# Longer load rows and a finer last weight piece in a decode kernel that streams 162 MB

## The chip, the cores and the metric

The kernel runs on one core of one Trainium2 chip. The metric is the device time of one execution in microseconds, lower is better.

## The reference, cut to what matters

One token goes through attention with a key/value cache and through a gated mixer, and a sigmoid gate blends the two.

```python
x = A_x                                   # 1 x 1 x 1024, bf16
q = x @ wq                                # wq 1024 x 4096: 32 heads of 128
p = softmax(q k^T / sqrt(128))            # k_cache 4 groups x 65536 x 128
a = (p @ v) @ wo                          # v_cache the same shape; wo 4096 x 1024
b = mixer(x; w_in 1024 x 3584, w_out 1792 x 1024)
out = g * a + (1 - g) * b
```

Keys and values are 67 MB each. With 28 MB of weights the core reads 162.0 MB once, and each byte is used for few operations. The loads set the time.

## The kernel before

The cache is cut into 16 tiles of keys and 16 of values, each 4 MB (128 partitions x 32 KB). On-chip memory holds three slots for key tiles and one double slot, `VB`, which in turn holds the query weights, the mixer weights, pairs of value tiles and output weights. All loads stand in one list, `stream`, and go to one hardware queue in this order. Offsets count 2-byte elements.

```python
SUB = 16384                       # one slot: 16384 elements, 32 KB a partition
GRAN = 2048                       # bookkeeping grain of the slots, in elements

load([("wq", 0)], rows(A_wq, 0, 8), VB)               # 64 KB a partition
...                                                   # keys 0, 1, mixer input (56 KB), keys 2, 3, mixer output
for i in range(6):
    load_k(2 * i + 4)
    load_v2(2 * i)                                    # a pair of value tiles, 64 KB a partition
    load_k(2 * i + 5)
load_v2(12)                                           # the seventh pair
load([("v", 14)], ...); load([("v", 15)], ...)        # into key slots
for i in range(3):
    load([("wo", i, 0)], rows(A_wo, i, 8), VB + 8 * DO * i)
s3 = kring()                                          # a key slot
for c0, c1 in [(0, 4), (4, 6), (6, 8)]:               # the last output weights, in eighths
    load([("wo", 3, c0)], rows(A_wo, 3, 8)[:, DO * c0:DO * c1], s3 + DO * c0)   # DO = 1024
```

A load is recorded as soon as every grain that it will overwrite has been used. It stops there if one has not, and `done` goes on when something more has been used:

```python
def grains(off, w):
    return list(range(off // GRAN, (off + w + GRAN - 1) // GRAN))

def issue():
    while issued[0] < len(stream):
        keys, off, src = stream[issued[0]]
        w = src.shape[1]
        gr = grains(off, w)
        if any(k not in used for x in gr if x in owner for k in owner[x]):
            return
        for x in gr:
            owner[x] = keys
        for c in range(0, w, SUB):                    # wider rows are cut: one load per 32 KB
            m = min(SUB, w - c)
            P("SP", lambda e, ...: e.dma_start(arena[:, o:o + m], src),
              w=[("slot", x) for x in grains(off + c, m)], dma="s%d" % grains(off + c, m)[0])
        issued[0] += 1

def done(key):
    used.add(key)
    issue()
```

`P` records an operation with the keys that it reads and writes and makes the semaphore waits from them. The attention loop takes a pair of value tiles per turn, and the output weights come last:

```python
for i in range(6):
    a = 2 * i + 4
    k_step(a, ...)                     # transpose (VectorE) and multiply (TensorE) a key tile
    pv_piece(2 * i)                    # TensorE: value tile, then done(("v", n))
    pv_piece(2 * i + 1)
    k_step(a + 1, ...)
...
for i, c0, c1 in [(0, 0, 8), (1, 0, 8), (2, 0, 8), (3, 0, 4), (3, 4, 6), (3, 6, 8)]:
    sl, keys = use(("wo", i, c0))
    ...                                # TensorE: 4 matmuls per eighth
    done(("wo", i, c0))
P("DVE", ...)                          # the sum to bf16, then the store
```

## Time and profile before

| | before |
|---|---|
| time, median of 5 (lowest to highest) | 383.73 us (383.66 to 383.97) |
| queue 1: packets, share of 16 engines | 6200, 98.8% |
| last weights landed | 379.50 us |
| busy TensorE, VectorE | 61%, 55% |

From the page of the kernel before: the DMA engines' busy tenths in 40 slices of the span and what they moved, the load queue and the instruction queue (packets, MB, share of 16 engines), and the group of the value matmuls (busy time, mean ns | idle time before them and what ended most of it).

```profile
DMA  9999999999999999999999999999999999999995
GB/s 384 439 435 425 423 417 435 439 436 433 439 425 418 432 430 439 439 432 432 429 420 429 435 439 434 429 435 426 422 432 437 435 432 429 439 425 420 423 425 220
...
q1 hardware_dynamic: 6200, 162.01, 98.8%
q8 instruction: 8, 0.13, 0.1%
...
L246 PE MATMUL obt<-arena 128*64 128x512 bf16 (+2 forms) x334 | 64.6, 428 | 30.6 <-DMA arena<-in_A_v_cache_dram 12.4
```

The queue is full to the last slice. TensorE waits 12.4 us for values, but that costs nothing while the queue stays full. In the packet records, 16 engines hold 16 packets on average from 1.0 us to the end of the stream.

The end of the chain of waits (start us, duration us, what):

```profile
351.47 28.03 DMA arena<-in_A_wo_dram
379.50 0.04 issue
379.54 0.63 PE fbt L706 x8
380.17 0.02 issue
380.19 0.42 DVE arena L712
```

The last piece was issued at 351.47 us and landed at 379.50. Eight matmuls and a cast follow. The queue's own waits (us in total, times, longest; the four largest sums):

```profile
SPq L365 <- PE obt L248: 234.1, 14, 29.8
SPq L365 <- DVE arena L476: 80.7, 6, 16.8
SPq L714 <- DVE arena L712: 28.7, 1, 28.7
SPq L365 <- PE mbt L535: 20.3, 3, 7.7
```

The sixth pair, tiles 10 and 11: its halves landed at 301.56 and 311.27 us. The timeline of TensorE shows the first matmuls of tile 10 and of tile 11, and the queue's timeline the issue of the seventh pair's first half with the three loads after it:

```profile
305.60 0.41 PE L246 MATMUL obt<-arena 128*64 128x512 bf16 x2
...
311.40 0.41 PE L246 MATMUL obt<-arena 128*64 128x512 bf16 x2 [2.16 <-DMA arena<-in_A_v_cache_dram]
```

```profile
309.28 8.77 SPq L365 DMA_DIRECT2D arena<-in_A_v_cache_dram  x4
```

Tile 10 took 3.48 us, from 305.60 to 309.08, where the next tile's first matmul could follow. The load that it frees room for was issued at 309.28, and its turn came at 318.69. (That is the first packet after as many bytes as all earlier loads have, counted in order of start. The engines are not in step: the first of them closed the load before it at 318.39.) It had some 9 us to spare. The stretches around it (start:end us, length, busy time and count of PE, PEld, DVE, ACT, POOL, then the granted TensorE clock, DMA share, GB/s):

```profile
306.00:311.00 5.00, 3.24 (x31) 0.69 (x12) 1.01 (x3) 0.00 (x0) 0.00 (x0) 1.00 0.98 419
311.00:314.00 3.00, 2.60 (x16) 0.86 (x10) 0.00 (x0) 0.00 (x0) 0.00 (x0) 0.65 1.06 459
314.00:317.00 3.00, 3.00 (x22) 0.96 (x10) 0.00 (x0) 0.00 (x0) 0.00 (x0) 0.78 0.96 415
```

### The profile page before, as it was taken

Reading aid. Unit: us, or ns where it says so; the run is one execution under the profiler, and the core shown is the slowest. Engines: PE = TensorE matmul, PEld = TensorE weight load, DVE = VectorE, ACT = ScalarE, POOL = GpSimd, SP = SyncE. Lnnn points to the kernel's source line nnn. Section 1 sums busy time; section 2 is a strip of 40 time slices with the busy share of each in tenths; the row PEclk is TensorE's granted clock in tenths of the full one; section 3 lists DMA queues with packets and bytes.
Section 4 is the critical chain, followed back from the end, with each engine's and each line's share of the span. In section 5 each row is a group of like instructions: output and inputs, shape, how many; then the busy total and the mean of one; then the engine's idle time right before and its main releaser. Section 6 shows DMA issues by size and latency. Waiting matters only on the chain.

```text
span 382.3 us, 2522 instructions
## 1 busy us (share of the span) xinstructions
PE 234.6 (61%) x1375; PEld 56.9 (15%) x785; DVE 211.7 (55%) x229; ACT 25.3 (7%) x39; POOL 1.5 (0%) x8
## 2 busy tenths in 40 slices
PE   0055754286687578545793777377938673849344
PEld 0011111111121111101120112012201121112121
DVE  6116952785781698067935980579448914842020
ACT  1000000102030001000210010001200100031000
POOL 1000000000000000000000000000000000000000
PEclk9996998689979599959898998786979988778695
DMA  9999999999999999999999999999999999999995
GB/s 384 439 435 425 423 417 435 439 436 433 439 425 418 432 430 439 439 432 432 429 420 429 435 439 434 429 435 426 422 432 437 435 432 429 439 425 420 423 425 220
DMA packets 6246, 162.16 MB, mean 424 GB/s; under 512 B 728, under 2 KB 732, under 8 KB 988
## 3 DMA queue, kind: packets, MB, share of 16 engines
q1 hardware_dynamic: 6200, 162.01, 98.8%
q8 instruction: 8, 0.13, 0.1%
q14 instruction: 2, 0.02, 0.0%
q10 hardware_dynamic: 36, 0.00, 0.0%
HBM read 162.01 MB, written 0.00 MB: 424 GB/s over the span
## 4 chain that ended last, share of the span: by engine, by line
DMA 61%; PE 19%; DVE 18%; SPq 1%; ACT 1%; issue 1%
DMA arena<-in_A_k_cache_dram 33%; DVE arena L476 13%; DMA arena<-in_B_w_in_dram 8%; DMA arena<-in_A_wo_dram 7%; DMA arena<-in_B_w_out_dram 6%; PE obt L246 6%; DMA arena<-in_A_wq_dram 6%; PE obt L248 5%; PE scp L246 4%; PE scp L248 4%; DVE arena L493 1%; SPq L365 1%; DVE arena L514 1%; DVE arena L464 1%; DVE arena L549 0%
## 5 line engine op out<-in xcount | busy, mean ns | idle before, releaser
L476 DVE STREAM_TRANSPOSE arena<-arena 128x2048 f32<-128x2048 f32 x64 | 145.5, 2295 | 84.5 <-DMA arena<-in_A_k_cache_dram 71.9
L246 PE MATMUL scp<-arena 128*128 128x512 bf16 x256 | 112.5, 439 | 83.4 <-DVE arena L476 61.0
L248 PE MATMUL scp<-arena 128*128 128x512 bf16 x256 | 111.0, 434 | 0.0
L246 PE MATMUL obt<-arena 128*64 128x512 bf16 (+2 forms) x334 | 64.6, 428 | 30.6 <-DMA arena<-in_A_v_cache_dram 12.4
L248 PE MATMUL obt<-arena 128*64 128x512 bf16 (+2 forms) x334 | 64.1, 424 | 0.0
L246 PEld LDWEIGHTS scp<-arena 128*128 128x128 bf16 x256 | 27.5, 107 | 192.2 <-DVE arena L476 93.8
L509 ACT ACTIVATE arena<-arena 128x1024 bf16<-128x1024 f32 x16 | 18.4, 1148 | 237.5 <-DVE arena L505 127.4
L246 PEld LDWEIGHTS obt<-arena 128*64 128x64 bf16 (+1 forms) x334 | 19.4, 116 | 86.6 <-issue 79.1
L493 DVE TENSOR_SCALAR_CACHE_REDUCE arena<-scp 128x1024 f32<-128x1024 f32 x16 | 19.3, 1205 | 9.3 <-PE scp L248 9.3
L514 DVE STREAM_TRANSPOSE arena<-arena 128x1024 bf16<-128x1024 bf16 x16 | 19.4, 1214 | 9.0 <-PE obt L248 6.4
L706 PE MATMUL fbt<-arena 128*1 128x256 bf16 x128 | 6.2, 339 | 5.9 <-DMA arena<-in_A_wo_dram 5.7
L539 DVE RECIPROCAL arena<-mbt 128x1 f32<-128x1 f32 x4 | 0.6, 139 | 14.0 <-PE mbt L535 14.0
L441 DVE CAST arena<-obt 97x1024 bf16<-97x1024 f32 x1 | 1.2, 1224 | 11.5 <-PE obt L248 11.5
L712 DVE CAST arena<-fbt 97x256 bf16<-97x256 f32 x1 | 0.4, 425 | 11.3 <-PE fbt L706 11.3
L588 DVE COPY arena<-obt 128x896 f32<-128x896 f32 x1 | 1.1, 1093 | 9.1 <-PE obt L248 9.1
L464 DVE COPY arena<-arena 32x32 bf16<-32x32 bf16 x16 | 2.7, 166 | 6.2 <-PE scp L248 6.0
L407 PE MATMUL scp<-arena 8*128 8x1 bf16 x8 | 0.6, 197 | 8.4 <-DVE arena L402 8.4
L706 PEld LDWEIGHTS fbt<-arena 128*1 128x1 bf16 x128 | 2.8, 93 | 8.8 <-DMA arena<-in_A_wo_dram 6.7
L595 ACT ACTIVATE arena<-arena 128x28 f32<-128x28 f32 x1 | 0.2, 226 | 52.4 <-DVE arena L594 52.4
L549 DVE SCALAR_TENSOR_TENSOR arena<-obt,arena 128x512 bf16<-128x512 f32 x4 | 3.0, 751 | 0.1
L601 PE MATMUL mbt<-arena 128*128 128x1 f32 x2 | 0.4, 260 | 4.3 <-DVE arena L600 4.3
L509 ACT ACTIVATION_READ_ACCUMULATOR arena<-arena 128x1 f32 x16 | 3.0, 186 | 0.0
(88 smaller groups left out, 47.0 us busy)
## 6 DMA issues: line engine op xcount, KB each, us to landing
arena<-in_A_k_cache_dram SPq DMA_DIRECT2D x16, 4096.0 KB, 38.4
arena<-in_A_v_cache_dram SPq DMA_DIRECT2D x16, 4096.0 KB, 31.1
arena<-in_A_wq_dram SPq DMA_DIRECT2D x2, 4096.0 KB, 16.8
arena<-in_A_wo_dram SPq DMA_DIRECT2D x3, 2048.0 KB, 22.6
arena<-in_B_w_in_dram SPq DMA_DIRECT2D x1, 4096.0 KB, 25.2
arena<-in_B_w_out_dram SPq DMA_DIRECT2D x1, 3584.0 KB, 23.1
arena<-in_B_w_in_dram SPq DMA_DIRECT2D x1, 3072.0 KB, 32.2
arena<-in_A_wo_dram SPq DMA_DIRECT2D x1, 1024.0 KB, 26.5
```

The costliest lines, as they stand in the source:

```text
L246: return e.matmul(*a, **kw)
L248: one = e.matmul(*a, **kw).ins
L365: P("SP", lambda e, o=OFF["RING"] + off + c, m=m, src=src[:, c:c + m]: e.dma_start(arena[:, o:o + m], src), w=[("slot", x) for x in grains ...
L441: P("DVE", lambda e: e.tensor_copy(psb[0:97, :], ob[0:97, :]), w=["psb", "ob"])
L464: P("DVE", lambda e, pb=pb: e.tensor_copy(vw(qpad, 24 + 32 * pb, [[QP, 4], [1, 8]], 32 * pb, 32), vw(qall, 8 * g, [[32, 4], [1, 8]], 32 * ...
L476: P("DVE", lambda e: e.transpose(ktb(i).bitcast(F32), sl[:, 4096 * p:4096 * (p + 1)].bitcast(F32)), r=keys[2 * p:2 * p + 2], w=[("kt", i % ...
L493: P("DVE", lambda e: e.tensor_scalar(scs(n), sc_ps(n), 0.0, None, op0=ALU.add, op1=ALU.max, accum_out=maxc[:, n:n + 1]), w=[("sc", n % NSC ...
L509: P("ACT", lambda e: e.activation(psb, scs(n), ACTF.Exp, bias=gcol(n // NP, K_NB), scale=SCALE, accum_out=lp[:, n:n + 1]), r=[("sc", n % N ...
L514: P("DVE", lambda e: e.transpose(ptsb(n), psb), r=["psb"], w=[("ptsb", n % 2)])
L549: P("DVE", lambda e: e.scalar_tensor_tensor(osc, ob[:, 512:1024], gcol(g, K_FB), osc, op0=ALU.mult, op1=ALU.add), r=[("fh", g, 1), "psb"], ...
L588: P("DVE", lambda e: e.tensor_copy(vw(zr, 0, [[FB4, 2], [32, FC], [1, 32]]), vw(ob, 0, [[512, 2], [1, FC], [FC, 32]])), w=[KZR, "ob"])
L706: ins = e.matmul(fb[32 * q:32 * q + 1, 0:QW], ovec[:, 8 * i + c:8 * i + c + 1], sl[:, o:o + QW], start=False, stop=(i == 3 and c == 7), ti ...
```

## The change

The intent is to make fewer packets, since each row of a load is one packet with some fixed cost, and to leave less TensorE work behind the last landing. Query weights, mixer input and six value pairs load as whole rows of 56 to 64 KB. The last output-weight piece of two eighths becomes two pieces of one.

```diff
-    for c0, c1 in [(0, 4), (4, 6), (6, 8)]:
+    for c0, c1 in [(0, 4), (4, 6), (6, 7), (7, 8)]:
         load([("wo", 3, c0)], rows(A_wo, 3, 8)[:, DO * c0:DO * c1], s3 + DO * c0)

+    whole = {("wq", 0), ("win", 0)} | {("v", 2 * i) for i in range(6)}
@@ issue()
-            for c in range(0, w, SUB):
-                m = min(SUB, w - c)
+            step = len(keys) * w if keys[0] in whole else SUB
+            for c in range(0, w, step):
+                m = min(step, w - c)
@@ the output weights
-    for i, c0, c1 in [(0, 0, 8), (1, 0, 8), (2, 0, 8), (3, 0, 4), (3, 4, 6), (3, 6, 8)]:
+    for i, c0, c1 in [(0, 0, 8), (1, 0, 8), (2, 0, 8), (3, 0, 4), (3, 4, 6), (3, 6, 7), (3, 7, 8)]:
```

## The prediction

> **What bounds the kernel.** The one load queue. The page shows queue 1 at 98.8% of the 16 DMA engines' span, 162.0 MB, 424 GB/s; DMA leads the chain of waits at 61%. In the packet records the engines hold nearly 16.0 packets at any time from 1.0 to 379.05 us: the queue never runs dry. The load issues agree: each waits 5 to 32 us in the queue behind earlier ones. Compute matters only where it delays an issue by more than that, and after the last landing at 379.5 us.
>
> **Costs.** Median packet times by row size: 4 KB 159 ns, 8 KB 312, 16 KB 614, 24 KB 915, 28 KB 1067, 32 KB 1216: a line of 0.0367 ns per byte plus about 11 ns. Sixteen engines at that slope move 435 GB/s, the fabric ceiling in the Trainium skill (DMA: Bandwidth & Descriptors, "Where 436 GB/s comes from"); the fixed part is of the kind in its "Why small descriptors are slow". The trace agrees with both. Packets overlap by some 3 ns; 4 MB follows 4 MB every 9.72 us, so the effective fixed cost is 9 to 10 ns a row.
>
> **Removed.** Query weights, mixer input and six pairs go from two packets per row to one: 1024 of 6200 packets, 64 per engine, x 9 to 10 ns = 0.6 us, all on the critical resource. This assumes that a 64 KB row travels as one packet of about 2418 ns (extrapolated). If it is cut into 32 KB, nothing is gained here.
>
> **Added.** The last output-weight rows are two of 2 KB instead of one of 4 KB: 8 more packets per engine, 0.1 us. Behind the last landing TensorE runs 4 matmuls instead of 8; before, the second four started 0.17 us after the first, so 0.17 us are saved.
>
> **Moved.** The first tile of a pair could be multiplied when its half had landed; now both wait for the pair (at most 9.7 us more), and the next pair is issued once, after both. A tile takes 3.45 us at full clock, up to 6.9 at half, so both need 7 to 14 us after the landing, with 19.4 us of other loads queued behind it: still 5 us or more ahead of need. The tightest place is the seventh pair (still in halves): before, its first half was issued at 309.3 us and started at 318.7. Now it follows the sixth pair's landing (311.3) by 3.5 to 5.5 us: 315 to 317, with about 1 us from issue to first packet (as at the start): 0.5 to 2.5 us to spare. Query and mixer weights need both halves anyway.
>
> **Sum.** 383.8 - 0.6 + 0.1 - 0.2 = about 383.1 us, range 382.4 to 383.9. Faster by over 2%: 1%; within 2%: 97%; slower: 2%.
>
> **What would show it.** Queue 1 with about 5200 packets; packets of 56 and 64 KB of about 2118 and 2418 ns; last landing near 378.9 us; 0.4 us of matmuls after it; DMA at nine tenths throughout; TensorE's waits for value loads grown from 12 us to some 30, at no cost; the seventh pair's first half issued near 315 us, without a gap in the packets near 318.
>
> **What would make it wrong.** Long packets running at another rate, or cut up (383.6 to 383.9); a gap where the seventh pair comes too late (1 to 3 us slower); a spread of completion between engines (2 us at the end before) that grows with long rows.

## More of the kernel before

The clock was 1.00 while tile 10 ran. It fell to 0.50 at 311.89, after 2.16 us in which TensorE was idle, and tile 11 ran at half clock until 315.31.

Where time and span are both listed, the time is 1.27 to 1.40 us longer than the span that the profile shows, so times are compared with times and traces with traces.

## The result, and the profile after

The changed kernel took 385.93 us, median of 5 (385.55 to 386.40), against 383.73 before. The ratio is 1.0057, 95% interval 1.0045 to 1.0069: slower by 2.2 us, where 0.6 us less had been forecast. A ratio is the mean time of one kernel's fast runs over that of the other's of the same rounds, so not quite the ratio of the medians.

The lines of the page of the changed kernel that answer to those shown before:

```profile
DMA  9989999999989999999999999999999999999993
GB/s 436 436 382 436 438 433 423 422 409 482 436 389 433 481 431 395 436 474 440 395 417 470 436 402 407 429 453 437 416 431 457 436 409 395 429 435 436 429 412 119
...
q1 hardware_dynamic: 5192, 162.01, 98.1%
q8 instruction: 8, 0.13, 0.1%
...
L246 PE MATMUL obt<-arena 128*64 128x512 bf16 (+2 forms) x334 | 67.5, 455 | 38.1 <-DMA arena<-in_A_v_cache_dram 29.2
```

There are 1008 packets fewer, as intended. The rates swing more from slice to slice; I take this for the coarser unit of a 64 KB packet, which no run tests. What stands out is the last slice: 119 GB/s instead of 220. The end of the chain of waits shows why:

```profile
349.16 29.04 DMA arena<-in_A_wo_dram
378.20 0.04 issue
378.24 0.60 PE fbt L708 x8
378.84 0.04 issue
378.88 0.41 PE fbt L708 x4
379.29 0.02 issue
379.31 2.67 DMA arena<-in_A_wo_dram
381.98 0.04 issue
382.02 0.41 PE fbt L708 x4
382.44 0.02 issue
382.46 0.42 DVE arena L714
```

The last load starts at 379.31 us, after the four matmuls of the eighth before it. It takes 2.67 us for 256 KB on a queue that is empty. The four largest sums of the queue's own waits name the wait, which the kernel before did not have:

```profile
SPq L367 <- PE obt L248: 211.6, 9, 37.0
SPq L367 <- DVE arena L478: 65.6, 6, 13.2
SPq L367 <- PE mbt L537: 59.2, 3, 28.2
SPq L367 <- PE fbt L708: 29.2, 1, 29.2
```

The reason stands in the code. An eighth is 1024 elements, a grain 2048. The seventh eighth begins at `s3 + 6144` and the last at `s3 + 7168`, which is the same grain. The owner of that grain is then the seventh eighth, and `issue()` returns until that has been used. The load is therefore recorded after the matmuls that read the grain, and on the chip it waits for them. The two pieces touch no common byte; only the bookkeeping joins them. Every earlier piece was a whole number of grains.

The sixth pair changed as well. These are the same views as before: TensorE's timeline, the queue's timeline, and the stretches.

```profile
310.74 0.64 PE L246 MATMUL obt<-arena 128*64 128x512 bf16 x2 [5.47 <-DMA arena<-in_A_v_cache_dram]
```

```profile
316.95 4.75 SPq L367 DMA_DIRECT2D arena<-in_A_v_cache_dram  x4
```

```profile
306.00:311.00 5.00, 0.26 (x2) 0.13 (x2) 0.61 (x3) 0.00 (x0) 0.00 (x0) 0.81 0.76 328
311.00:314.00 3.00, 3.00 (x16) 0.73 (x8) 0.00 (x0) 0.00 (x0) 0.00 (x0) 0.50 0.99 426
314.00:317.00 3.00, 3.00 (x22) 0.62 (x10) 0.00 (x0) 0.00 (x0) 0.00 (x0) 0.68 1.01 437
```

TensorE stood idle for 5.47 us until the whole pair had landed. Its clock was then 0.50, and tile 10 took 6.01 us instead of 3.48. The seventh pair's first load was issued at 316.95, and by the same count of bytes its turn came at 318.34. The first engine had closed key tile 15 at 317.90, only 0.95 us after the issue. Some engines then stood idle (0.11 us per engine on average between 316.5 and 320.5 us), and several packets that started between 317.96 and 318.57 us took 1.5 to 1.9 us instead of 1.22.

Landings of the same load in both traces show how the gain came and went (us from the span's start; a load has landed with the last of its 16 completions, read here as one from each of the 16 engines):

| load | before | after | difference |
|---|---|---|---|
| key tile 15, the last before the seventh pair | 320.98 | 320.40 | -0.58 |
| value tile 13, the second half of the seventh pair | 340.40 | 339.83 | -0.57 |
| value tile 14 | 350.12 | 349.88 | -0.24 |
| value tile 15 | 359.84 | 359.59 | -0.25 |
| output weights, eighths 5 and 6 of the last part | 378.26 | 378.20 | -0.06 |
| last output weights | 379.50 | 381.98 | +2.48 |

So 0.58 us were saved, more than half of it was lost after 340 us, and 2.5 us came at the very end. Near 318 us no landing was late. There it was the first of the 16 completions that fell back: at key tile 15 it came 0.51 us earlier than in the kernel before, at the next load 0.10 us.

### The profile page after: what moved, and what is told of

It reads as the page before. It is cut to its first block, busy times and chain, and to the rows that moved or that the text cites. A ratio compares the mean times of both kernels' runs of the same rounds, so it can differ in the third digit from the quotient of the medians.

```text
span 384.6 us, 2507 instructions
## 1 busy us (share of the span) xinstructions
PE 230.3 (60%) x1375; PEld 55.4 (14%) x785; DVE 211.2 (55%) x229; ACT 25.3 (7%) x39; POOL 1.5 (0%) x8
## 3 DMA queue, kind: packets, MB, share of 16 engines
q1 hardware_dynamic: 5192, 162.01, 98.1%
## 4 chain that ended last, share of the span: by engine, by line
DMA 76%; PE 18%; DVE 4%; issue 0%; ACT 0%; ACTq 0%; SPq 0%
DMA arena<-in_A_v_cache_dram 39%; DMA arena<-in_A_k_cache_dram 11%; PE obt L246 8%; DMA arena<-in_A_wo_dram 8%; PE obt L248 8%; DMA arena<-in_B_w_in_dram 8%; DMA arena<-in_B_w_out_dram 6%; DMA arena<-in_B_b_sp_dram 5%; DVE arena L478 2%; PE fbt L708 0%; DVE arena L516 0%; ACT arena L511 0%; DVE arena L495 0%; ACTq L271 0%; SPq L367 0%
## 5 line engine op out<-in xcount | busy, mean ns | idle before, releaser
L246 PE MATMUL scp<-arena 128*128 128x512 bf16 x256 | 105.8, 413 | 72.2 <-DVE arena L478 60.2
L248 PE MATMUL scp<-arena 128*128 128x512 bf16 x256 | 104.7, 409 | 0.0
L246 PE MATMUL obt<-arena 128*64 128x512 bf16 (+2 forms) x334 | 67.5, 455 | 38.1 <-DMA arena<-in_A_v_cache_dram 29.2
L248 PE MATMUL obt<-arena 128*64 128x512 bf16 (+2 forms) x334 | 66.9, 452 | 0.0
L246 PEld LDWEIGHTS scp<-arena 128*128 128x128 bf16 x256 | 26.2, 102 | 173.3 <-DVE arena L478 94.0
```

What stands on the lines that cost most here:

```text
L246: return e.matmul(*a, **kw)
L248: one = e.matmul(*a, **kw).ins
```

## The experiments

Theory A: the shared grain delays the last load, and that is the loss. Rival B: the long rows, or the later release of pairs, cost the time. Four kernels ran, 5 rounds each, with the kernel before at 383.70 us (383.56 to 384.24).

**Long rows without the finer tail (e1_rows_only).** The whole change, but with the old pieces:

```diff
-    for c0, c1 in [(0, 4), (4, 6), (6, 7), (7, 8)]:
+    for c0, c1 in [(0, 4), (4, 6), (6, 8)]:           # and the same in the loop that uses them
```

> The change with the last output-weight pieces put back to 4, 2, 2 eighths. Theory A (the last eighth shares a 2048-element bookkeeping grain with the seventh, so its load is issued only after the seventh is multiplied): the loss goes, and the long rows show their own worth, 0.6 us of saved fixed cost less about 0.3 us for the short gap before the seventh pair: 383.3 to 383.6 us, last landing near 379.2 us. Theory B (long rows, or the later release of the pairs, cost the time): it stays near 385.9 us.

Measured: 383.67 us (383.02 to 384.95, six executions), ratio 1.0000 (0.9987 to 1.0013). The loss is gone, so B falls. The gain that A expected did not show in the median, which missed the forecast by a little, and the spread of 1.9 us asked for a reason of its own.

**The finer tail without long rows (e2_tail_only).** The kernel before, with the pieces 4, 2, 1, 1.

> The kernel before with nothing but the last output-weight pieces in 4, 2, 1, 1 eighths. Theory A: the last load is issued after the seventh eighth's matmuls, some 2.6 us after the other six, and lands 2.7 us after that: 385.9 to 386.5 us, the queue waiting about 29 us for the matmuls of the output weights. Theory B: 383.6 to 383.8 us, no such wait.

Measured: 385.99 us (385.97 to 386.14), ratio 1.0059 (1.0047 to 1.0071). The queue's own waits of this run have the line again:

```profile
SPq L365 <- PE fbt L706: 28.7, 1, 28.7
```

The tail alone makes the whole loss.

**The whole change, last eighth in its own grain (e3_tail_apart).**

```diff
-        load([("wo", 3, c0)], rows(A_wo, 3, 8)[:, DO * c0:DO * c1], s3 + DO * c0)
+        load([("wo", 3, c0)], rows(A_wo, 3, 8)[:, DO * c0:DO * c1], s3 + DO * (8 if c0 == 7 else c0))
```

> The whole change, with the last eighth put 2048 elements further on, into a bookkeeping grain of its own (the space is free), nothing else. Theory A: all output-weight loads are issued together near 350 us, the last lands near 379.2 us, and the time is 383.1 to 383.5 us. Theory B: 385.9 us as before this edit.

Measured: 383.73 us (383.27 to 384.10), ratio 0.9998 (0.9986 to 1.0010). The line for the output matmuls is gone from the queue's waits, and the last weights landed at 379.43 us. Moving one piece by 2048 elements takes the loss away. The time is a little above the forecast range of 383.1 to 383.5, as it was in e1.

**The finer tail alone, last eighth in its own grain (e4_tail_only_apart).** The edit of e3, on the kernel of e2.

> The kernel before with the pieces 4, 2, 1, 1 and the last eighth in a grain of its own. What the finer tail is worth without the accident: 0.17 us less TensorE after the last landing, 0.08 us more for 8 rows per engine: 383.5 to 383.75 us, no change that 5 rounds can show. If smaller rows at the end cost more than their 9 to 10 ns (for instance a fixed cost per load), it is over 383.9 us.

Measured: 383.59 us (383.53 to 383.93), ratio 0.9997 (0.9985 to 1.0009). Against e2 the shared grain cost 2.40 us (385.99 - 383.59). Whether the finer tail is worth its forecast tenth of a microsecond, 5 rounds don't tell.

That settled the loss. Open was why the long rows gained nothing. Theory C: they save about 0.6 us, but the sixth pair's later release makes the seventh pair's load too late. Rival D: long rows are worth nothing. Again with the kernel before at 383.69 us (383.50 to 383.89).

**Five long pairs instead of six (e5_five_pairs).** As e3, with `range(5)` in `whole`, so that the sixth pair loads as halves.

> As the run with the last eighth apart, but the sixth pair (tiles 10 and 11) loads as two halves again, so only five pairs are long rows. Theory C (six whole pairs save 0.6 us, but the seventh pair's first load is then issued only about 1 us before it is needed, at a granted clock of 0.5 during tile 10, and the queue runs dry for 0.3 to 1 us, differently in each execution): no gap near 318 us, that load issued near 310 to 313 us, spread below 0.5 us, 383.0 to 383.3 us, 0.3 to 0.7 us under the other run of this call. Theory D (long rows are worth nothing on the clock): 383.6 to 383.8 us, as with six pairs.

Measured: 383.08 us (383.02 to 383.36), ratio 0.9985 (0.9972 to 0.9999). The load is issued early again, even ahead of the 310 to 313 us expected:

```profile
308.93 8.75 SPq L367 DMA_DIRECT2D arena<-in_A_v_cache_dram  x4
```

The median is 0.27 us under that with six pairs (next run), a little less than the 0.3 to 0.7 us that C forecast, and the two intervals overlap. The gain over the kernel before, 0.61 us, is about what the saved rows and the finer tail are worth; D is outside its range.

**Six long pairs once more (e6_tail_apart_2).** The kernel of e3.

> The run with the last eighth apart and six long pairs once more, for a comparison in the same rounds and a second trace. 383.3 to 384.1 us with the same spread of about 0.8 us; the seventh pair's first load issued at 316.5 to 318 us, and a gap near 318 us, under both theories.

Measured: 383.35 us (383.18 to 383.65), ratio 0.9992 (0.9979 to 1.0004). The spread was smaller than expected. In the profiled execution the load was issued at 316.19 us, ahead of the 316.5 to 318 expected, and waited 2.04 us for its turn: no gap there. I had expected one in this trace, so the gap is a matter of tenths of a microsecond in each execution.

**The sixth pair alone as long rows (e7_pair6_only).** The kernel before with `whole = {("v", 10)}`.

> The kernel before with the sixth pair alone as long rows. Theory C: 8 rows per engine saved, 0.08 us, against the gap: 383.8 to 384.5 us with a wider spread than before's. Theory D: 383.7 us, no gap.

Measured: 384.32 us (383.59 to 385.16), ratio 1.0015 (1.0002 to 1.0027). Eight rows per engine fewer, and slower with a spread of 1.6 us, as C forecast. But the interval only just excludes no loss, and the same kernel later (e11) does not confirm it. The trace also says that not all of this is the gap: the landing of key tile 15 was already 0.38 us behind that of the kernel before (321.36 against 320.98 us), ahead of the late load, and the last landing 0.68 us (380.18 against 379.50).

**All loads as rows of 16 KB (e8_rows_16k).**

```diff
-            for c in range(0, w, SUB):
-                m = min(SUB, w - c)
+            for c in range(0, w, SUB // 2):
+                m = min(SUB // 2, w - c)
```

> The kernel before with every load cut at 16 KB rows, each piece a load of its own: 296 more packets per engine, nothing waits for later data than before. At 9 to 10 ns a row: 2.7 to 3.0 us more, 386.4 to 386.8 us; queue 1 never dry. If the fixed cost of a row is hidden where the queue is deep: 383.7 to 384.3 us.

Measured: 386.60 us (386.57 to 386.65), ratio 1.0076 (1.0064 to 1.0089). 2.91 us for 296 rows more on each engine: 9.8 ns a row. Since each piece is a load of its own, 37 completion packets more per engine (median 9 ns) are in that figure; over all 333 packets it is 8.7 ns each. The fixed cost is real on a full queue.

What made tile 10 slow? The Trainium skill says (TensorE: Matmul & The Clock Gate, "What's actually happening") that the clock falls to half after at least one idle window of about 3.4 us, and that the window runs free (the traces bear out the length, not that the window must be idle; see the last section). That would make the wait for the whole pair, 5.5 us, the cause of the half clock (Theory E). Rival F: the load is late because of the later landing itself. The test keeps TensorE busy during the wait. The kernel before had 383.75 us (383.47 to 384.25).

**The sixth pair alone, TensorE kept busy (e9_warm_pair6).** Ahead of `pv_piece(10)`:

```diff
+    def keep_warm(m):                                  # m = 24, result unused
+        j = (nkt[0] - 1) % NKT
+        def f(e):
+            for x in range(m):
+                ins = mm(e, x > 0, sc_ps(15)[:, 0:512], qpad[:, 0:128], ktb(j)[:, 0:512],
+                         start=True, stop=True, skip_group_check=True)
+            return ins
+        P("PE", f, r=["qpad", ("kt", j)], w=[KSC(15)])
```

> The kernel with the sixth pair alone as long rows, plus 24 matmuls whose result nobody uses (they write the score bank of tile 15 before its first real matmul clears it) put before tile 10's multiplication, so that TensorE is busy for about 5.2 us of the 5.5 us in which it waits for the whole pair. Theory E (the wait for the whole pair lets the granted clock fall to 0.5, tile 10 then takes about 6 us instead of 3.45, and this alone makes the next load too late): the clock stays at 1.0 from 306 to 315 us, tile 10 takes 3.5 us, the seventh pair's first load is issued near 315 us, no gap near 318 us, 383.5 to 383.7 us with a spread under 0.4 us, against about 384.3 us without. Theory F (the later issue comes of the wait for the landing itself, whatever the clock): issue at 316 us or later, gap and 383.8 to 385 us as before.

Measured: 383.72 us (383.70 to 383.80), ratio 1.0000 (0.9987 to 1.0014). This is just above E's range, and with the added work the spread was 0.10 us. The stretches and the queue's timeline of this run:

```profile
306.00:311.00 5.00, 4.66 (x22) 0.00 (x0) 0.81 (x3) 0.00 (x0) 0.00 (x0) 1.00 0.93 400
311.00:314.00 3.00, 2.60 (x24) 0.80 (x14) 0.00 (x0) 0.00 (x0) 0.00 (x0) 1.00 1.06 459
314.00:317.00 3.00, 3.00 (x30) 0.81 (x14) 0.00 (x0) 0.00 (x0) 0.00 (x0) 1.00 0.91 393
```

```profile
315.09 4.73 SPq L367 DMA_DIRECT2D arena<-in_A_v_cache_dram  x4
```

The clock stayed at 1.00, tile 10 took 3.48 us, and the load was issued at 315.09 us, in time.

**Six long pairs, TensorE kept busy (e10_warm_six).** The same 24 matmuls in the kernel of e3.

> Six long pairs, the last eighth apart, and the same 24 unused matmuls. Theory E: as with five pairs, 383.0 to 383.1 us, spread under 0.4 us, no gap near 318 us. Theory F: 383.3 to 383.8 us with a gap in some executions.

Measured: 383.30 us (383.15 to 383.48), ratio 0.9990 (0.9977 to 1.0002). No gap, spread 0.33 us, load issued at 314.84 us. The median is 0.2 us above E's forecast, at the lower edge of F's, and above what five pairs gave. Nor is it clearly under six pairs without the added matmuls (383.35 in e6, 383.73 in e3). I have no reason for that; the times do not show what the clock is worth with six pairs.

**The sixth pair alone again (e11_pair6_again).** The kernel of e7, for the comparison in the same rounds.

> The sixth pair alone as long rows, without the added matmuls, in the same rounds as the comparison: 383.6 to 385.2 us, median about 384.3, under both theories.

Measured: 384.04 us (383.49 to 384.42), ratio 1.0005 (0.9993 to 1.0018), so 0.3 us above e9, with a spread of 0.93 against 0.10 us. The intervals of the two overlap, so it is the traces that must decide. The same stretches in its profile:

```profile
306.00:311.00 5.00, 0.00 (x0) 0.00 (x0) 0.72 (x3) 0.00 (x0) 0.00 (x0) 0.70 0.87 374
311.00:314.00 3.00, 2.85 (x14) 0.67 (x8) 0.00 (x0) 0.00 (x0) 0.00 (x0) 0.50 1.14 492
314.00:317.00 3.00, 3.00 (x26) 0.74 (x12) 0.00 (x0) 0.00 (x0) 0.00 (x0) 0.87 0.89 382
```

The same wait without the added matmuls, and the clock is at 0.50. The traces side by side, worked out from the packet and instruction records: tile 10's matmuls, the issue of the seventh pair's first load, its wait for its turn (by the count of bytes), and the engine time lost there (idle engine time between 316.5 and 320.5 us plus the excess of packets over the usual time between 316 and 321 us, per engine).

```
                    tile 10 starts, takes   issue    waits   loss   time of that execution
before                 305.60   3.48        309.28    9.42   0.00   -
five pairs             305.24   3.48        308.93    9.19   0.00   383.08
kept warm, pair 6      311.40   3.48        315.09    3.52   0.01   383.71
kept warm, six         311.16   3.48        314.84    3.36   0.00   383.30
six, again             311.00   4.98        316.19    2.04   0.04   383.18
pair 6, again          311.15   5.25        316.61    2.05   0.10   383.49
six, tail apart        311.21   5.75        317.16    1.14   0.47   383.35
the change             310.74   6.01        316.95    1.38   0.43   385.93
pair 6 alone           311.70   5.77        317.67    1.19   0.52   384.32
rows only              310.98   6.45        317.63    1.02   0.67   383.87
```

A load issued with some 2 us left costs at most 0.1 us of engine time. With 1.4 us or less it costs 0.43 to 0.67 us, in idle engines (0.11 to 0.39 us) and in packets that run longer (0.28 to 0.32 us; why they do is not shown). Where tile 10 takes 3.48 us, there is no loss, whether it starts at 305 or at 311 us. So what makes the load too late is the clock (E), not the landing alone (F). How long tile 10 takes varies from 4.98 to 6.45 us with where the windows of half clock lie, which fits a window that runs free.

Engine time lost is not yet kernel time. The engines are some 2 us apart, and a landing is the last of 16 completions. Near 318 us it is the engines ahead that lose: in the changed kernel the first and the last completion of a load lay 2.03 us apart at key tile 15 and 1.63 us at the next load. From key tile 15 to eighths 5 and 6 of the last output weights, landings fell back against the kernel before by 0.52 us in the changed kernel, 0.78 in rows only, 0.25 in pair 6 alone and only 0.04 in six with the tail apart, and by 0.02 us at most in the traces with 2 us or more left. They fell back in the stretches in which the instruction queue moved a packet, near 344 and 372 us. That these packets then meet engines which have no lead left is read from the order in time, not tested. So a late load takes away a lead, and that became time in three of four traces.

## Why the prediction was wrong, point by point

**What bounds the kernel: right.** Time followed the packets, as e8 shows.

**The saved rows: right.** The prediction said 64 rows x 9 to 10 ns = 0.6 us, with 64 KB rows of about 2418 ns. Queue 1 shows 5192 packets (forecast about 5200). Those of 64 KB took 2420 ns (median), those of 56 KB 2116. The first completion of key tile 15 came 0.51 to 0.62 us earlier in all five traces with six long pairs. That its landing was 0.58 us earlier in the changed kernel is partly luck: in the other four it was 0.09 to 0.33 us, because the last engine decides. e8 measured 9.8 ns a row, and five pairs gained 0.61 us (383.69 - 383.08; 56 rows, and the finer tail).

**The step that failed.** "The last output-weight rows are two of 2 KB instead of one of 4 KB: 8 more packets per engine, 0.1 us." This counted the new load as one more in a full queue, and "last landing near 378.9 us" rests on it. In its place there was a new wait: the last load was issued only after the matmuls of the piece before it, at 379.31 us instead of some 351, and landed 2.67 us later on an empty queue. e2 and e4 put the price at 2.40 us. It could have been read from the code without a profile: 1024-element pieces against `GRAN = 2048`. The prediction costed the packets of the new piece and never asked whether its issue condition was still met. The Trainium skill (DMA: Bandwidth & Descriptors, "Anatomy of one DMA — SWDGE (gpsimd) path") gives about 2.0 us plus bytes / 436 GB/s for one load issued from GpSimd, which this one is not; for 256 KB that is an estimate of 2.6 us, close to the 2.67 measured here. Taken out of the full queue, the load cost the kernel 2.40 us of it.

**A term that was mis-sized.** "Now it follows the sixth pair's landing (311.3) by 3.5 to 5.5 us: 315 to 317 [...] 0.5 to 2.5 us to spare." The place was right, the size was not: in the six traces with the wait and no added matmuls tile 10 took 4.98 to 6.45 us, the issue followed the pair's landing by 5.2 to 6.7 us and came at 316.19 to 317.67 us, and 0.43 to 0.67 us of engine time were lost in four of them. The prediction knew that half clock doubles the time of a tile, but not that the wait it had just introduced was what halves the clock. The traces of e9 and e10 show that it was. The 17 us that TensorE waited more for values (29.2 against 12.4, forecast "some 30, at no cost") cost nothing that e5 would show in five pairs; in the sixth they used up the time to spare.

**The smaller tail: open.** Behind the last landing, the chain before shows 0.69 us to the cast (380.19 - 379.50), after it 0.48 (382.46 - 381.98): 0.21 us less in the traces, where 0.17 were forecast, but 5 rounds of e4 don't resolve it against its 8 rows more.

**What stays open.** The forecast of busy loads "at nine tenths throughout" failed in the last slice, for the reason given; the eight tenths in two earlier slices, with no gap in the packet records, I take for the coarser packets. In the traces with a loss of 0.47 us or more near 318 us, the last 4 KB packets were slower by 0.2 to 0.4 us per engine on average (e1, e3, e7). I have not found why. The changed kernel's other 0.2 us, between value tile 15 and the last pieces but one, fall where the 16 completions of a load move from 1.98 to 2.17 us apart, after an instruction packet at 371.85 us; that is not tested either. A risk that the prediction named did not show: at key tile 15 the completions lay 2.03 to 2.63 us apart with six long pairs, and 2.11 to 2.57 us in the three traces with rows of 32 KB at most.

**The better version.** Five long pairs with the last eighth in its own grain (e5) ran at 383.08 us, 0.15% under the kernel before, and its interval just excludes no gain.

## What to carry to other kernels

When a load is cut finer, check what decides when it may be issued (grain, slot, semaphore) before counting its packets: one load that left a full queue cost 2.40 us here, nearly its whole round trip of 2.67. Merging loads delays what waits for their first part; look for the one place where the next load is nearly due, and size it with the clock that the longer wait will leave. Look at the last of the 16 completions as well as at the mean: a gap on engines that are ahead need not cost time. Row length itself is a small lever once rows reach 32 KB: some 10 ns out of 1216.

## What the Trainium skill lacked or had wrong

- DMA: Bandwidth & Descriptors, "Where 436 GB/s comes from": its ceiling of 435 GB/s agrees. The slope over the median packets of 2 to 64 KB, 0.0368 ns per byte on each of 16 engines, is 435 GB/s. "Why small descriptors are slow" gives some 3 cycles of fixed overhead per packet; if these are cycles of the 850 MHz fabric, which the page does not say, that is about 3.5 ns (an estimate). Measured on a full queue: 9.8 ns a row (e8; 8.7 ns a packet with the completions counted), or 8 to 13 ns in the packets' own times, from 2 KB (84 ns) to 64 KB (2420 ns).
- DMA: Bandwidth & Descriptors, "Latency and other measured facts": about 0.6 us to the first byte on this path. Here the first packet started 0.95 us after the issue of the last load on an idle queue (1.0 us at the start of the kernel), and 1.4 us ahead of need, by the count of bytes, was too late.
- TensorE: Matmul & The Clock Gate, "What's actually happening": the length of the window agrees, the condition does not. The half-clock stretches were 3.41 us or a multiple of it. But its table has the clock fall after at least one idle window, and here the window need not be idle. Cut into windows of 3.413 us by the clock records, the 13 traces show the clock fall after 213 windows in which TensorE was busy for 0 to 51% of the time, stay at 1.00 after 753 with 42 to 100%, and rise again after 200 with 76 to 100%. In the kernel before it fell at 311.89 us after a window with 1.25 us of matmuls. What the page lacks is the indirect price in a load-bound kernel: the slower matmuls cost nothing themselves, but released a buffer 1.5 to 3.0 us later (tile 10 took 4.98 to 6.45 us instead of 3.48), and up to 0.67 us of engine time was lost to the load stream.
- Runtime: NRT & Kernel Launch, "Instruction fetch mechanics": instruction memory is refilled in 16 KiB blocks, and the cost of crossing one is called mostly hidden; no page says what a refill costs a load stream. The page of the profile shows eight such packets in queue 8. In the packet records of the kernel before each took 1.0 to 1.1 us. The 16 completions of a load lay 0.46 to 0.61 us apart before the first of them (44 us) and 1.9 to 2.2 us apart after it, to the end; that the one makes the other is read from the order in time, not tested, and the step is more than the one packet took.
